# Activation of the last chunk by halves, and q of blocks 3, 5 and 7 transposed by VectorE and two trips through memory

## The chip, the core and the metric

One core of a Trainium2 chip runs the whole program. The metric is the device time of one execution in microseconds (us); the median of three runs of the kernel before is 1563.25 us.

## What is computed

Linear attention over 8 batches of 8 heads, 576 positions each, and then two dense blocks on its 4608 tokens, all in float32:

```python
q_s = exp(q - max(q, -1)); q_s = q_s / (sum(q_s, -1) + 1e-09)      # over the 64 columns of a head
k_s = exp(k - max(k,  2)); k_s = k_s / (sum(k_s,  2) + 1e-09)      # over the positions
attn = einsum('bhsd,bhde->bhse', q_s, einsum('bhsd,bhse->bhde', k_s, v))
x = attn.transpose(0, 2, 1, 3).reshape(4608, 512)
g = relu(x @ w_in) ** 2;  x = g @ w_out                            # first layer, 512 -> 2048 -> 512
h = x @ w2_in;  g = where(h > 0, h, exp(min(h, 0)) - 1);  out = g @ w2_out   # second layer
```

## The kernel before

Tokens go through the first layer in nine blocks of 512 (numbers 0 to 8). A block is *prepared* (its q normalised, transposed, multiplied with the small k-v products of its batches), then its *up* products are computed (16 chunks j, 12 matmuls each), while the preparation of the next block runs beside them in small steps. From block 1 on two blocks form a pair: after the second (even) block's up products follows the pair's *down* product, by a scheme with seven products of quarters instead of eight, cut into 56 *units* of 6 matmuls. A unit u reads its weights from a tile `w1_<t>_<u>` (line 743), which SyncE (SP) loads from the tensors `w1s` in DRAM. Those are written during blocks 1 and 2 by ScalarE and VectorE steps `s_hi` and `s_lo`, whose results `shwo`, `slwo` go out by DMAs on GpSimd's queue (lines 203 and 216), eight groups of four, the group of quarter 3 last. Every float32 operand is split into a high and a low part (ScalarE writes the high one, VectorE the difference: `uh`, `ul` for units, `dh`, `dl` in the second layer), and each product takes three matmuls.

The order is written out by hand. `attention(t)` lists the steps of a block's preparation in numbered slots 0 to 31; `place_all` spreads those slots over the up chunks and units in which they run. For an odd block t, slots 0 and 1 run in the last chunk of block t-2, slots 2 to 22 in chunks 0 to 13 of block t-1, and slots 23 to 31 in units 11 to 21 of the pair t-2, t-1. In q's preparation `q_load` brings 128 tokens, `q_max` to `q_norm` normalise them, `x_tr` transposes them on TensorE (four 128x128 transposes per two heads, line 399, into PSUM), ScalarE copies the result out to `qt` (line 408), and `x_mm` multiplies it with the k-v products (line 427). Tiles come from pools with a given number of buffers; which buffer a new tile gets, and so what its first writer waits for, is settled when the program is built.

In the second layer, tokens go in groups n = 0 to 4 (512, 512, 512, 384 and 384 columns per half). A group's up stage (line 926) leaves its values in eight chunks m, each with rows r = 0 and 1 and two sides; `elu_1` to `elu_5` apply the activation to both sides of a row at once. Then follows the down stage (line 1031): for each step q `d_mm` runs two products, `t2_sum` forms differences of quarters, and `d_split` cuts the operand for step q + 2. The differences T3 and T1 of the last two chunks (number 3) feed the steps 6 and 7.

Of the kernel before, what the change touches and what calls it, by code (L numbers as in the profile page):

```python
# [8 lines left out]
F32 = mybir.dt.float32  # L9
# [3 lines left out]
AF = mybir.ActivationFunctionType  # L13
# [3 lines left out]
P = 128  # L17
# [3 lines left out]
def tile_attention_moe_moe2(  # L21
# [18 lines left out]
    nc = tc.nc  # L40
    NT, DM = q.shape
    B, NP, _, S = kt_dram.shape
    SC = v.shape[3]
    NFC = wi0.shape[0]
    D = 64
    H = DM // D
    TB = 512
    NB = NT // TB
    NS = TB // P
    LAG = 2  # L50
    NSL = 2 * NFC
    PAIRED = 1
# [6 lines left out]
    att = att_pool.__enter__()  # L59
# [7 lines left out]
    dram = ctx.enter_context(tc.tile_pool(name="dram", bufs=1, space=bass.MemoryType.DRAM))  # L67

    x2d = [dram.tile([NP, P, TB], F32, name=f"x2d{t}") for t in range(NB)]
    NG, HW = NFC // 2, DM // 2  # L70
    w2s = [dram.tile([P, 7, 2, HW], F32, name=f"w2s{j}") for j in range(NG)]
    w1s = [dram.tile([P, 7, 2, HW], F32, name=f"w1s{j}") for j in range(NG)]
    w3s = [dram.tile([P, 7, 2, HW], F32, name=f"w3s{j}") for j in range(NG)]

    keep.tile([P, 32], F32, tag="even", name="even")
    ident = att.tile([P, P], F32, tag="ident", name="ident")
# [9 lines left out]
    def xf_slot(i, name):  # L86

        return keep.tile([P, 2 * TB], F32, tag=f"xf{i}", name=name)
# [137 lines left out]
    st = {}  # L226
# [105 lines left out]
    def kv_inv(b, p):  # L332
        z = st["kz", b, p]
        nc.vector.reciprocal(z, z)

    def q_load(t, s):
        qr = att.tile([P, H, D], F32, tag="q", bufs=4, name=f"q{t}_{s}")
        r = t * TB + s * P
        nc.sync.dma_start(qr.rearrange("p h d -> p (h d)"), q[r : r + P, :])
        st["q", t, s] = qr  # L340

    def per_head(ap):
# [45 lines left out]
    def pieces(t):  # L388
        lo, hi = t * TB, (t + 1) * TB
        while lo < hi:  # L390
            b = lo // S
            n = min(hi, (b + 1) * S) - lo
            yield b, lo - t * TB, n
            lo += n

    def x_tr(t, p):
        pt = bank([P, TB], f"pt{t}_{p}")
# [51 lines left out]
    def plan():  # L449
        slots = [[] for _ in range(NSL)]  # L450

        def put(i, f, *a):
            slots[i].append((f, a))

        return slots, put

    def attention(t):

        slots, put = plan()
        new = [b for b, _, _ in pieces(t) if b not in begun]  # L460
        begun.update(new)

        far = t > 1
        for b in new:
            for p in range(NP):
                for i, f in (
                    (0, kt_load), (2, k_max), (5, k_load), (5, v_load), (8, k_row), (8, k_sub), (9 + far, k_exp),
                    (11 + far, kv_mm), (11 + far, kv_sum), (11 + far, kv_inv), (11 + 2 * far, kv_out),
                ):
                    if p == NP - 1 and (f is kv_out if far else i == 11):  # L470
                        i = 12
                    put(i + 4 * p, f, b, p)
        for s in range(NS):
            put(s // 2, q_load, t, s)
            for i, f in (
                (2, q_max), (3, q_sub), (4 + far, q_exp), (5 + 2 * far, q_sum), (6 + 2 * far, q_eps),
                (7 + 2 * far, q_inv), (7 + 2 * far, q_norm),
            ):
                put(i + 5 * s, f, t, s)
        turns = ((25, 28), (26, None), (29, 31), (30, None)) if far else ((25, 27), (26, None), (28, 29), (28, None))  # L480
        for p, (i, j) in enumerate(turns):
            if j is not None:
                put(j, x_mm, t, p)
            put(i, x_tr, t, p)
        return slots
# [305 lines left out]
    def u_out(t, i, side, half, block, m):  # L791

        o = parts_y[i][m]
        nc.vector.tensor_tensor(o, o, accs[side, m], op=ALU.add)
        nc.gpsimd.dma_start(x2d[block][2 * half + m], o)
# [40 lines left out]
    SIZES = (512, 512, 512, 384, 384)  # L836
# [101 lines left out]
    acc, part, g2, es = {}, {}, {}, {}  # L938
# [12 lines left out]
        nc.scalar.activation(p, acc[CHAIN[i], m], AF.Copy)  # L951
        part[i, m] = p

    def rows(m, r):
        return g2[r, m // 2][:, m % 2].rearrange("p s t -> p (s t)")

    def h_part(n, m, r, side, i, add):
# [6 lines left out]
        else:  # L964
            nc.vector.tensor_tensor(h, part[add, m], acc[CHAIN[i], m], op=ALU.add)

    def elu_1(n, m, r):


        e = pool2.tile([P, 2 * SIZES[n]], F32, tag="e", bufs=2, name=f"e{n}_{m}_{r}")  # L970
        nc.scalar.activation(e, rows(m, r), AF.Relu, scale=-1.0)
        es[m, r] = e

    def elu_2(n, m, r):
        e = es[m, r]
        g = pool2.tile([P, 2 * SIZES[n]], F32, tag="g", bufs=2, name=f"t{n}_{m}_{r}")
        nc.scalar.activation(g, e, AF.Tanh, scale=-0.5)
        es[m, r] = e, g

    def elu_3(n, m, r):  # L980
        e = es[m, r][0]
        nc.scalar.activation(e, e, AF.Exp, scale=-1.0)

    def elu_4(n, m, r):
        e, g = es[m, r]
        nc.vector.scalar_tensor_tensor(g, e, 1.0, g, ALU.add, ALU.mult)  # L986

    def elu_5(n, m, r):
        g, h = es.pop((m, r))[1], rows(m, r)
        nc.vector.scalar_tensor_tensor(h, h, 0.0, g, ALU.max, ALU.add)  # L990


# [76 lines left out]
    def second_layer():  # L1069


        nonlocal pool2
        for m in range(2):
            u_out(NB - 2, 4, 0, 1, NB - 2, m)
        early2.tile([P, 56], F32, tag="even", name="even")
        layer_pool.__exit__(None, None, None)
        square_pool.__exit__(None, None, None)
        pool2 = ctx.enter_context(tc.tile_pool(name="pool2", bufs=1, reuse_waits="tile"))
        last = len(SIZES) - 1
        for n in range(last + 1):  # L1080
            steps = {}

            def put(key, f, *a):
                steps.setdefault(key, []).append((f, (n, *a)))

            evict = {
                0: (keep_part, 0), 3: (keep_part, 3), 2: (keep_part, 2), 1: (h_part, 0, 0, 1, 0),
                6: (h_part, 0, 1, 6, 2), 4: (h_part, 1, 1, 4, 3), 5: (h_part, 1, 0, 5, None),
            }
            for at, m, i in ORDER:  # L1090
                put(at, evict[i][0], m, *evict[i][1:])
            if n:
                put(1, lambda n: d_out(n - 1, 4, 0, 1, 0))
            for m in range(NG):
                for x, (to, f, r) in enumerate((
                    (6, elu_1, 0), (7, elu_2, 0), (8, elu_3, 0), (9, elu_4, 0), (10, elu_5, 0), (10, elu_1, 1),
                    (11, elu_2, 1), (12, elu_3, 1), (13, elu_4, 1), (14, elu_5, 1),
                )):
                    put(7 * m + to if m < NG - 1 else ("d", (0, 0, 0, 1, 1, 1, 2, 2, 3, 3)[x]) if x else 56, f, m, r)
            for k in range(3):  # L1100
                put(14 * k + 22, t2_sum, "T3", k)
                put(14 * k + 25 if k < 2 else ("d", 0), t2_sum, "T1", k)
            put(30, d_split, 0)
            put(39, d_split, 1)
            put(54, d_split, 2)
            for q, f, *a in (
                (4, t2_sum, "T3", 3), (5, t2_sum, "T1", 3),
                (6, d_keep, 4, 0, "e"), (8, d_v), (10, t2_sum, "T2", 0), (11, t2_sum, "T2", 1),
                (12, d_keep, 0, 0, "g"), (12, t2_sum, "T2", 2), (13, t2_sum, "T2", 3), (16, d_keep, 6, 1, "g"),
                (19, t2_sum, "T4", 0), (20, d_out, 6, 0, 0, 1), (21, d_out, "v", 0, 1, 1), (22, t2_sum, "T4", 1),  # L1110
                (23, t2_sum, "T4", 2), (24, t2_sum, "T4", 3), (25, d_out, 0, 1, 0, 0),
            ):
                put(("d", q), f, *a)
            if n < last:
                for q, f, a in (
                    (6, x2_sum, "T3"), (7, x2_sum, "T1"), (9, x2_split, 0), (14, x2_sum, "T2"), (15, x2_split, 1),
                    (16, x2_split, 6), (17, x2_split, 2), (18, x2_split, 3), (25, x2_sum, "T4"), (26, x2_split, 4),
                    (27, x2_split, 5),
                ):
                    steps.setdefault(("d", q), []).append((f, (n + 1, a)))  # L1120
                for k, (side, h) in enumerate(((0, 0), (1, 0), (1, 1), (0, 1))):
                    steps.setdefault(35 + 2 * k, []).append((x2_load, (n + 1, h, side)))
            for at, m, i in ORDER:
                take(n, m, i)
                run(steps.get(at, ()))
            for q in range(NU // 2):
                d_mm(n, 2 * q)
                d_mm(n, 2 * q + 1)
                run(steps.get(("d", q), ()))
                if 0 < q < NU // 2 - 2:  # L1130
                    d_split(n, q + 2)
        d_out(last, 4, 0, 1, 0)
# [6 lines left out]
    def run(steps):  # L1139
        for f, a in steps:  # L1140
            f(*a)
# [3 lines left out]
    with tc.manual_schedule():  # L1145
# [25 lines left out]
        x = attention(PAIRED + 1)  # L1171
# [3 lines left out]
        for t in range(PAIRED, NB - 2, 2):  # L1175
            seconds = [(t, "s", s) for s in range(NU // 2)]
            x = attention(t + 2)
# [3 lines left out]
            x = attention(t + 3)  # L1181
# [14 lines left out]
        at = 0  # L1196
# [14 lines left out]
        at = 0  # L1211
# [134 lines left out]
```

## Time and profile before

| | |
|---|---|
| median of three runs | 1563.25 us (1563.06 to 1564.92) |
| profiled execution, its own time | 1561.17 us |
| span of its instructions | 1559.0 us |
| TensorE (PE) busy | 1533.3 us, 98% |
| VectorE (DVE) busy | 1227.1 us, 79% |
| ScalarE (ACT) busy | 1013.2 us, 65% |
| GpSimd (POOL) busy | 129.3 us, 8% |
| transfers | 351.66 MB, mean 226 GB/s |

The profile names an instruction by its line, engine and operation, and by the tiles it writes and reads. Idle time is put down to whatever the instruction behind it waited for.

### The profile page before, as it was taken

The numbers are of one execution on the slowest core, as the hardware profiler recorded it, in microseconds if no ns is written. First come the engines' busy times: TensorE is split into PE (matmuls) and PEld (weight loads), VectorE is DVE, ScalarE is ACT, GpSimd is POOL, SyncE is SP. The second block draws the span as 40 slices with busy tenths as digits, with TensorE's granted clock in tenths as the row PEclk, the third lists the DMA queues.
The fourth block names the chain that finished last, engine by engine and source line by source line (L and its number), as shares of the span: only waits on it lengthen the run. The fifth ranks groups of instructions, "written<-read, shape, count | busy, mean of one in ns | idle before, by whom it ended". The sixth has DMA issues, their size and how long they took to land.

```text
span 1559.0 us, 25506 instructions
## 1 busy us (share of the span) xinstructions
PE 1533.3 (98%) x9056; PEld 1321.1 (85%) x9056; DVE 1227.1 (79%) x1793; ACT 1013.2 (65%) x1606; POOL 129.3 (8%) x202
## 2 busy tenths in 40 slices
PE   7999999999999999999999999999999999999999
PEld 5778777878778787787888889988998899999998
DVE  8998597787778787885686888688868886887876
ACT  7886655577565765656564876387538853864863
POOL 1002220032011310032201000000000000000000
PEclk9999999999999999999999999999999999999999
DMA  9857566677586775855686776877686768888876
GB/s 268 244 168 257 203 220 210 225 256 259 152 273 212 266 227 170 265 183 186 215 272 204 206 233 179 241 202 237 179 241 194 231 180 250 275 256 281 261 237 206
DMA packets 200765, 351.66 MB, mean 226 GB/s; under 512 B 20160, under 2 KB 67264, under 8 KB 200640
## 3 DMA queue, kind: packets, MB, share of 16 engines
q1 hardware_dynamic: 186096, 302.71, 64.1%
q0 software_dynamic: 14400, 47.20, 7.6%
q8 instruction: 73, 1.20, 0.3%
q14 instruction: 52, 0.43, 0.1%
q10 hardware_dynamic: 144, 0.13, 0.0%
HBM read 287.05 MB, written 62.91 MB: 224 GB/s over the span
## 4 chain that ended last, share of the span: by engine, by line
PE 75%; DVE 10%; issue 6%; ACT 5%; DMA 3%; POOL 1%; SPq 0%; ACTq 0%; DVEq 0%; POOLq 0%
PE p L926 21%; PE y L1031 17%; PE p L765 16%; PE ph L648 6%; PE ph L649 6%; PE ph L650 6%; DVE dl L1012 2%; ACT dh L1011 1%; DMA kt<-kt_dram 1%; DVE ul L753 1%; PE px L427 1%; DVE g L990 1%; PE pk L307 1%; DVE t L986 1%; PE pt L399 1%
## 5 line engine op out<-in xcount | busy, mean ns | idle before, releaser
L1031 PE MATMUL y<-w,dh 128*128 128x256 f32 x2016 | 359.2, 281 | 0.0
L926 PE MATMUL p<-x2h,w 128*128 128x512 f32 (+1 forms) x1120 | 321.6, 367 | 0.0
L1031 PEld LDWEIGHTS y<-w,dh 128*128 128x128 f32 x2016 | 309.7, 188 | 0.1
L1031 PE MATMUL y<-w,dl 128*128 128x256 f32 x1008 | 285.1, 283 | 4.9 <-DVE dl L1012 4.7
L765 PE MATMUL p<-uh,w 128*128 128x512 f32 x896 | 282.6, 392 | 0.3 <-DMA w<-w1s 0.3
L648 PE MATMUL ph<-xh,wi0h 128*128 128x512 f32 x576 | 229.5, 399 | 0.0
L926 PEld LDWEIGHTS p<-x2h,w 128*128 128x128 f32 x1120 | 207.1, 188 | 26.1
L650 PE MATMUL ph<-xh,wi0l 128*128 128x512 f32 x576 | 224.8, 390 | 2.6 <-DVE wi0l L149 2.6
L649 PE MATMUL ph<-xl,wi0h 128*128 128x512 f32 x576 | 225.1, 391 | 0.7 <-DVE xl L586 0.6
L926 PE MATMUL p<-x2l,w 128*128 128x512 f32 (+1 forms) x560 | 205.5, 367 | 0.0
L765 PEld LDWEIGHTS p<-uh,w 128*128 128x128 f32 x896 | 168.2, 188 | 37.1 <-issue 1.5
L1031 PEld LDWEIGHTS y<-w,dl 128*128 128x128 f32 x1008 | 189.7, 188 | 8.0 <-DVE dl L1012 7.8
L1011 ACT ACTIVATE dh<-g 128x1024 fp32r<-128x1024 f32 (+1 forms) x120 | 115.8, 973 | 114.0 <-PE y L1031 101.2
L752 ACT ACTIVATE uh<-B 128x512 fp32r<-128x512 f32 x192 | 120.4, 631 | 93.7 <-PE p L765 70.3
L765 PE MATMUL p<-ul,w 128*128 128x512 f32 x448 | 176.4, 394 | 2.0 <-DVE ul L753 1.6
L753 DVE TENSOR_TENSOR ul<-B,uh 128x512 fp32r<-128x512 f32 x192 | 129.5, 688 | 47.1 <-ACT uh L752 46.4
L1012 DVE TENSOR_TENSOR dl<-g,dh 128x1024 fp32r<-128x1024 f32 (+1 forms) x120 | 133.8, 1116 | 39.1 <-ACT dh L1011 38.8
L657 ACT ACTIVATE B<-ph 128x512 f32<-128x512 f32 x128 | 76.3, 596 | 120.6 <-PE ph L650 116.8
L648 PEld LDWEIGHTS ph<-xh,wi0h 128*128 128x128 f32 x576 | 109.0, 189 | 28.4 <-issue 3.9
L650 PEld LDWEIGHTS ph<-xh,wi0l 128*128 128x128 f32 x576 | 108.2, 188 | 27.3 <-DVE wi0l L149 4.1
L649 PEld LDWEIGHTS ph<-xl,wi0h 128*128 128x128 f32 x576 | 108.2, 188 | 22.7 <-DVE xl L586 1.8
L926 PEld LDWEIGHTS p<-x2l,w 128*128 128x128 f32 x560 | 105.1, 188 | 13.0
(155 smaller groups left out, 2279.8 us busy)
## 6 DMA issues: line engine op xcount, KB each, us to landing
w<-w2s SPq DMA_DIRECT2D x280, 256.0 KB, 3.2
w<-w3s SPq DMA_DIRECT2D x280, 256.0 KB, 3.0
w<-w1s SPq DMA_DIRECT2D x224, 256.0 KB, 3.8
raw_wo<-wo_dram SPq DMA_DIRECT2D x32, 512.0 KB, 4.6
vr<-v_dram SPq DMA_DIRECT2D x32, 320.0 KB, 5.6
kt<-kt_dram SPq DMA_DIRECT2D x32, 288.0 KB, 4.0
q<-q_dram SPq DMA_DIRECT2D x36, 256.0 KB, 4.5
ks<-k_dram SPq DMA_DIRECT2D x28, 320.0 KB, 4.6
```

The costliest lines, as they stand in the source:

```text
L307: nc.tensor.matmul(pk[j * D : (j + 1) * D], ks[:, c, j * D : (j + 1) * D], vr[:, c, j * (D + 1) : (j + 1) * (D + 1)], start=(c == 0), stop ...
L648: nc.tensor.matmul(ph, hi[:, c], xh[p], start=(p == 0), stop=False)
L649: nc.tensor.matmul(ph, hi[:, c], xl[p], start=False, stop=False)
L650: nc.tensor.matmul(ph, lo[:, c], xh[p], start=False, stop=(p == NP - 1))
L657: nc.scalar.activation(g, ph, AF.Relu)
L752: nc.scalar.activation(hi, x, AF.Copy)
L753: nc.vector.tensor_tensor(lo, x, f32(hi), op=ALU.subtract)
L765: nc.tensor.matmul(accs[side, m], w[:, s, m], x, start=(new and (j, s) == (0, 0) and x is hi), stop=(j == NG - 1 and s == 1), skip_group_c ...
L926: nc.tensor.matmul(acc, w[:, s, c], x[:, k], start=(begin and (k, s) == (0, 0) and x is hi), stop=((k, s) == (1, 1)), skip_group_check=not ...
L1011: nc.scalar.activation(hi, x, AF.Copy)
L1012: nc.vector.tensor_tensor(lo, x, f32(hi), op=ALU.subtract)
L1031: nc.tensor.matmul(y2[side, b][:, a * HW : (a + 1) * HW], x[:, u % 2, at], w[:, s], start=(new and (j, s, a) == (0, 0, 0) and x is hi), st ...
```

## The change

The last chunk's activation is split: in chunk 7 row 1 is taken in two halves, first the side that T3 needs, then the other one; row 0 stays whole. T3 and T1 of the last chunks are formed two steps earlier. In blocks 3, 5 and 7 the 16 transposes on TensorE and the four copies out of PSUM are gone. VectorE turns 32x32 squares of each normalised quarter into the tile `q<t>` (written with a step of four elements), four DMAs of 32 partitions each put that tile into a DRAM tensor `qd<t>` in the order wanted, and two DMAs read it back into the buffers xf0 and xf1. Quarters are loaded with every fourth token, in buffers that the `qt` tiles have otherwise (two instead of four), and each step of q's preparation runs earlier, so that the last quarter is done in chunk 12 of the even block.

```diff
+    TURNED = range(PAIRED + 2, NB, 2)
+    qd = {t: dram.tile([2, 2, P, TB], F32, name=f"qd{t}") for t in TURNED}
...
     def q_load(t, s):
...
+        rows = q[t * TB : (t + 1) * TB]
+        if t in TURNED:
+            qr = att.tile([P, H, D], F32, tag="qt", bufs=2, name=f"q{t}_{s}")
+            rows = rows.rearrange("(p s) c -> s p c", s=NS)[s]
+        else:
+            qr = q_tile(t)[:, s * DM : (s + 1) * DM].rearrange("p (h d) -> p h d", d=D)
+            rows = rows[s * P : (s + 1) * P]
+        nc.sync.dma_start(qr.rearrange("p h d -> p (h d)"), rows)
...
+    def q_turn(t, s):
+        turned = q_tile(t).rearrange("p (g t s) -> p g t s", g=2 * H, s=NS)[:, :, :, s]
+        nc.vector.transpose(turned, st.pop(("q", t, s)).rearrange("p h (j d) -> p (h j) d", j=2))
+
+    def q_store(t):
+        n = D // 2
+        for i in range(P // n):
+            rows = qd[t].rearrange("h u (r d) n -> d (h u r) n", d=n)[:, :, i * P : (i + 1) * P]
+            nc.gpsimd.dma_start(rows, q_tile(t)[i * n : (i + 1) * n].rearrange("p (g n) -> p g n", n=P))
+
+    def q_rows(t, half):
+        x = xf_slot(half, f"qt{t}_{half}").rearrange("p (u n) -> p u n", u=2)
+        nc.gpsimd.dma_start(x, qd[t][half].rearrange("u p n -> p u n"))
...
+            if t in TURNED:
+                at = (0, 4, 9, 13)[s]
+                put((0, 0, 8, 12)[s], q_load, t, s)
+                for i, f in (
+                    (2, q_max), (3, q_sub), (4, q_exp), (6, q_sum), (7, q_eps), (7, q_inv), (8, q_norm), (8, q_turn),
+                ):
+                    put(at + i, f, t, s)
+                continue
...
+        if t in TURNED:
+            put(21, q_store, t)
+            for half in range(2):
+                put(24, q_rows, t, half)
+                put(29 + 2 * half, x_mm, t, 2 * half)
+            return slots
...
-                    put(7 * m + to if m < NG - 1 else ("d", (0, 0, 0, 1, 1, 1, 2, 2, 3, 3)[x]) if x else 56, f, m, r)
+                    if m < NG - 1:
+                        put(7 * m + to, f, m, r)
+                    elif r:
+                        put((55, 55, 56, ("d", 0), ("d", 0))[x - 5], f, m, r, 1)
+                        put(("d", (1, 2, 2, 4, 4)[x - 5]), f, m, r, 0)
+                for to, f in zip((0, 0, 0, 1, 1), (elu_1, elu_2, elu_3, elu_4, elu_5)):
+                    if m == NG - 1:
+                        put(("d", to), f, m, 0)
...
-                (4, t2_sum, "T3", 3), (5, t2_sum, "T1", 3),
+                (2, t2_sum, "T3", 3), (3, t2_sum, "T1", 3),
```

On GpSimd's queue, at the end of block 2, the DMAs `w1s<-shwo` and `w1s<-slwo` of groups 2 and 3 (the last of the eight) stand so in the kernel before, and after them the next pair's results:

```order
L203 DMA w1s_100<-shwo_2_2_2388 128x2x256
L216 DMA w1s_100<-slwo_2_2_2391 128x2x256
L203 DMA w1s_101<-shwo_3_1_2499 128x2x256
L216 DMA w1s_101<-slwo_3_1_2502 128x2x256
L203 DMA w1s_101<-shwo_3_2_2528 128x2x256
L216 DMA w1s_101<-slwo_3_2_2531 128x2x256
L795 DMA x2d_82<-k_1_0_2713 128x512
```

The same place now, with block 3's four stores to `qd` and its two reads:

```order
L205 DMA w1s_100<-shwo_2_2_2392 128x2x256
L218 DMA w1s_100<-slwo_2_2_2395 128x2x256
L416 DMA qd_114<-q_2202 32x16x128 x4
L205 DMA w1s_101<-shwo_3_1_2507 128x2x256
L218 DMA w1s_101<-slwo_3_1_2510 128x2x256
L205 DMA w1s_101<-shwo_3_2_2534 128x2x256
L218 DMA w1s_101<-slwo_3_2_2537 128x2x256
L420 DMA qt_0_2765<-qd_114 128x2x512
L420 DMA qt_1_2767<-qd_114 128x2x512
```

The four stores have moved in ahead of the four DMAs of group 3, whose last one unit 3 of the first pair reads.

On SP, the loads of the weights of units 2 to 6 of that pair, with the semaphores that each waits for, before:

```order
L743 DMA w_1_2_2534<-w1s_100 128x512 [waits DMASW6_49,DMASW5_49,DMASW7_49,DMASW1_49,DMAHW6_49,DMASW0_49,DVE_49]
L743 DMA w_1_3_2536<-w1s_101 128x512 [waits DMASW3_49,DMASW2_49,DMASW4_49,DMASW1_49,DMAHW7_49,DMASW0_49,DVE_49]
L743 DMA w_1_4_2577<-w1s_102 128x512 [waits DMAHW0_49,PE_49]
L743 DMA w_1_5_2579<-w1s_103 128x512 [waits DMAHW1_49]
L743 DMA w_1_6_2581<-w1s_104 128x512 [waits DMAHW2_49,PE_49]
```

And now:

```order
L785 DMA w_1_2_2540<-w1s_100 128x512 [waits DMASW6_49,DMASW5_49,DMASW7_49,DMASW1_49,DMAHW6_49,DMASW0_49,DVE_49]
L785 DMA w_1_3_2542<-w1s_101 128x512 [waits DMAHW6_49,DMASW7_49,DMAHW7_49,DMASW6_49,PE_49]
L785 DMA w_1_4_2583<-w1s_102 128x512 [waits DMAHW0_49]
L785 DMA w_1_5_2585<-w1s_103 128x512 [waits DMAHW1_49]
L785 DMA w_1_6_2587<-w1s_104 128x512 [waits DMAHW2_49]
```

The load for unit 3 had a buffer that a `shwo` tile left; in the new program its tile lies at the address of unit 2's tile, and the load waits for unit 2's load and for TensorE (DMAHW6 and PE) besides the two stores it reads.

On VectorE, at the start of a down stage of the second layer (group 0; `t_7_r`, `g` are the activation of the last chunk, `dl_q` the low part for step q), before:

```order
L1004 TENSOR_TENSOR g_0_2_9219<-g_0_2_9219 128x2x512
L986 SCALAR_TENSOR_TENSOR t_7_0_9558<-e_7_0_9526,t_7_0_9558 128x1024
L990 SCALAR_TENSOR_TENSOR g_0_3_9402<-g_0_3_9402,t_7_0_9558 128x1024
L1012 TENSOR_TENSOR dl_3_9595<-g_0_0_8881,dh_3_9594 128x1024
L1012 TENSOR_TENSOR dl_4_9630<-g_0_1_9044,dh_4_9629 128x1024
L986 SCALAR_TENSOR_TENSOR t_7_1_9626<-e_7_1_9592,t_7_1_9626 128x1024
L990 SCALAR_TENSOR_TENSOR g_0_3_9403<-g_0_3_9403,t_7_1_9626 128x1024
L1012 TENSOR_TENSOR dl_5_9666<-g_0_2_9219,dh_5_9665 128x1024
L1004 TENSOR_TENSOR t_0_3_9697<-g_0_3_9403,g_0_3_9402 128x1024
L1012 TENSOR_TENSOR dl_6_9700<-t_0_3_9697,dh_6_9699 128x1024
```

And now:

```order
L1030 SCALAR_TENSOR_TENSOR t_7_1_9458<-e_7_1_9456,t_7_1_9458 128x512
L1034 SCALAR_TENSOR_TENSOR g_0_3_9343<-g_0_3_9343,t_7_1_9458 128x512
L1048 TENSOR_TENSOR g_0_2_9159<-g_0_2_9159 128x2x512
L1030 SCALAR_TENSOR_TENSOR t_7_0_9505<-e_7_0_9503,t_7_0_9505 128x1024
L1034 SCALAR_TENSOR_TENSOR g_0_3_9342<-g_0_3_9342,t_7_0_9505 128x1024
L1056 TENSOR_TENSOR dl_3_9542<-g_0_0_8821,dh_3_9541 128x1024
L1048 TENSOR_TENSOR t_0_3_9576<-g_0_3_9343,g_0_3_9342 128x1024
L1056 TENSOR_TENSOR dl_4_9579<-g_0_1_8984,dh_4_9578 128x1024
L1048 TENSOR_TENSOR g_0_3_9342<-g_0_3_9342 128x2x512
L1056 TENSOR_TENSOR dl_5_9614<-g_0_2_9159,dh_5_9613 128x1024
```

Two instructions of half size now stand ahead of `dl_3`, and the differences T3 and T1 (the L1048 rows behind it) come two steps of `dl` earlier than they did.

## Rows read from the trace of the kernel before

**Rows 1.** The page: busy time, share of the span and instructions of each engine.

```profile
PE 1533.3 (98%) x9056; PEld 1321.1 (85%) x9056; DVE 1227.1 (79%) x1793; ACT 1013.2 (65%) x1606; POOL 129.3 (8%) x202
```

**Rows 2.** Waits of PE: who waited for whom, us in total, times, longest.

```profile
PE y L1031 <- DVE dl L1012: 4.7, 12, 0.5
...
PE p L765 <- DMA w<-w1s: 0.3, 1, 0.3
```

**Rows 3.** Line 399: count, ns min/median/max, first and last start.

```profile
L399 PE MATMUL pt<-ident,q x128: 271/272/328, 99.5 to 715.1; 128*128 128x128 f32 x128
```

**Rows 4.** Timeline of PE around eight transposes: start, us, engine, line, operation.

```profile
257.04 0.39 PE L765 MATMUL p<-uh,w 128*128 128x512 f32 x1
257.27 1.04 PE L399 MATMUL pt<-ident,q 128*128 128x128 f32 x8
...
258.38 0.40 PE L765 MATMUL p<-ul,w 128*128 128x512 f32 x1
```

**Rows 5.** Waiting chain at the first pair's start, in order of time.

```profile
224.81 2.51 DMA w1s<-slwo
...
227.85 2.80 DMA w<-w1s
...
230.78 9.38 PE p L765 x40
```

**Rows 6.** Timeline of POOL there: first and last of four DMAs.

```profile
221.66 0.72 POOL L203 DMA_DIRECT2D w1s<-shwo  x1 [7.99 <-ACT shwo L202]
...
224.81 0.74 POOL L216 DMA_DIRECT2D w1s<-slwo  x1
```

**Rows 7.** Timeline of PE there: last matmul of unit 2.

```profile
230.09 0.39 PE L765 MATMUL p<-uh,w 128*128 128x512 f32 x1
```

**Rows 8.** Groups by line and form: busy us, mean ns of one, idle before.

```profile
L216 POOL DMA_DIRECT2D w3s<-slwo x24 | 17.5, 730 | 15.1 <-DVE slwo L215 7.7 <-DVE sumswo L175 6.8 <-issue 0.2
...
L795 POOL DMA_DIRECT2D x2d<-k x18 | 10.0, 554 | 223.6 <-DVE k L794 222.8 <-issue 0.3
...
L352 DVE TENSOR_TENSOR q<-q,qm 128x512 f32<-128x512 f32 x32 | 21.9, 684 | 0.2
...
L1004 DVE TENSOR_TENSOR g<-g,g 128x1024 f32<-128x1024 f32 x24 | 29.3, 1219 | 0.1
```

**Rows 9.** Timeline of DVE in block 2: instructions behind idle time.

```profile
191.16 0.69 DVE L661 TENSOR_TENSOR B<-B 128x512 f32<-128x512 f32 x1 [2.29 <-ACT B L657]
...
208.36 0.69 DVE L215 TENSOR_TENSOR slwo<-sumswo,shwo 128x512 fp32r<-128x512 f32 x1 [0.86 <-ACT shwo L202]
...
221.29 0.69 DVE L215 TENSOR_TENSOR slwo<-sumswo,shwo 128x512 fp32r<-128x512 f32 x1 [0.17 <-ACT shwo L202]
```

**Rows 10.** The page: DMA issues, count, KB each, us to landing.

```profile
vr<-v_dram SPq DMA_DIRECT2D x32, 320.0 KB, 5.6
...
q<-q_dram SPq DMA_DIRECT2D x36, 256.0 KB, 4.5
ks<-k_dram SPq DMA_DIRECT2D x28, 320.0 KB, 4.6
```

**Rows 11.** Timeline of DVE, first down stage of the second layer.

```profile
925.74 1.23 DVE L990 SCALAR_TENSOR_TENSOR g<-g,t 128x1024 f32<-128x1024 f32 x1
926.88 1.22 DVE L1012 TENSOR_TENSOR dl<-g,dh 128x1024 fp32r<-128x1024 f32 x1
```

**Rows 12.** Timeline of PE in the same stage: steps 3 and 6.

```profile
928.39 0.28 PE L1031 MATMUL y<-w,dl 128*128 128x256 f32 x1
...
936.75 0.39 PE L1031 MATMUL y<-w,dh 128*128 128x256 f32 x2
937.60 0.39 PE L1031 MATMUL y<-w,dl 128*128 128x256 f32 x1 [0.45 <-DVE dl L1012]
```

**Rows 13.** Timeline of PE in group 3's down stage: step 3.

```profile
1379.75 0.39 PE L1031 MATMUL y<-w,dh 128*128 128x256 f32 x2
1380.24 0.39 PE L1031 MATMUL y<-w,dl 128*128 128x256 f32 x1
```

More of the change, by code (lines that the diff above doesn't have):

```diff
@@ L334, in kv_inv, with q_tile @@
         nc.vector.reciprocal(z, z)
+    def q_tile(t):
+        if ("all", t) not in st:
+            st["all", t] = att.tile([P, NS * DM], F32, tag="q", name=f"q{t}")
+        return st["all", t]
     def q_load(t, s):
-        qr = att.tile([P, H, D], F32, tag="q", bufs=4, name=f"q{t}_{s}")
-        r = t * TB + s * P
-        nc.sync.dma_start(qr.rearrange("p h d -> p (h d)"), q[r : r + P, :])
+        rows = q[t * TB : (t + 1) * TB]
[6 more added lines that the diff above has]
+        nc.sync.dma_start(qr.rearrange("p h d -> p (h d)"), rows)
         st["q", t, s] = qr
@@ L394, in pieces @@
             lo += n
+    def q_turn(t, s):
[9 more added lines that the diff above has]
+        nc.gpsimd.dma_start(x, qd[t][half].rearrange("u p n -> p u n"))
+        for i in range(2):
+            st["qt", t, 2 * half + i] = x[:, i]
     def x_tr(t, p):
@@ L952, in keep_part, with rows @@
         part[i, m] = p
-    def rows(m, r):
+    def rows(m, r, *side):
+        if side:
+            return g2[r, m // 2][:, m % 2, side[0]]
         return g2[r, m // 2][:, m % 2].rearrange("p s t -> p (s t)")
@@ L965, in h_part, with elu_1, elu_2, elu_3 @@
             nc.vector.tensor_tensor(h, part[add, m], acc[CHAIN[i], m], op=ALU.add)
[L967 to L976, printed above, removed]
+    def elu_1(n, m, r, *side):
+        e = pool2.tile(list(rows(m, r, *side).shape), F32, tag="e", bufs=2, name=f"e{n}_{m}_{r}")
+        nc.scalar.activation(e, rows(m, r, *side), AF.Relu, scale=-1.0)
+        es[m, r, *side] = e
+    def elu_2(n, m, r, *side):
+        e = es[m, r, *side]
+        g = pool2.tile(list(rows(m, r, *side).shape), F32, tag="g", bufs=2, name=f"t{n}_{m}_{r}")
         nc.scalar.activation(g, e, AF.Tanh, scale=-0.5)
-        es[m, r] = e, g
-    def elu_3(n, m, r):
-        e = es[m, r][0]
+        es[m, r, *side] = e, g
+    def elu_3(n, m, r, *side):
+        e = es[m, r, *side][0]
         nc.scalar.activation(e, e, AF.Exp, scale=-1.0)
-    def elu_4(n, m, r):
-        e, g = es[m, r]
+    def elu_4(n, m, r, *side):
+        e, g = es[m, r, *side]
         nc.vector.scalar_tensor_tensor(g, e, 1.0, g, ALU.add, ALU.mult)
-    def elu_5(n, m, r):
-        g, h = es.pop((m, r))[1], rows(m, r)
+    def elu_5(n, m, r, *side):
+        g, h = es.pop((m, r, *side))[1], rows(m, r, *side)
         nc.vector.scalar_tensor_tensor(h, h, 0.0, g, ALU.max, ALU.add)
```

## The prediction, as it was put on record before the run

> **What bounds the kernel now.** I read the page's table of engines first: TensorE (PE) is busy in 98% of the span, VectorE (DVE) in 79%, ScalarE (ACT) in 65%, GpSimd (POOL) in 8% [rows 1]. Then PE's waits: nearly all of what the trace calls waiting there is 12 times 0.4 us for a `dl` of DVE in the second layer's down stages, and once 0.3 us for a weight load, the one of unit 3 of the first pair [rows 2]. So nothing is gained by relieving an engine other than PE. A gain comes from work that leaves PE or from those two waits; a loss comes from a new wait of PE. The sum has three terms: the transposes, the activation by halves, and what the new work on DVE, POOL and the queues does to PE.
>
> **Term 1, the transposes.** Eight blocks have 128 of them, 16 a block [rows 3], so three blocks lose 48. The 271 ns of a row is latency, since they overlap. What they take from the stream is seen between neighbours: the matmul ahead starts at 257.04 and the first transpose at 257.27, so a matmul of 512 columns takes a step of 0.23; from the first transpose to the next matmul are 1.11 us [rows 4], and 1.11 less one such step is 0.88 for eight, 0.11 us each (the last step counted as a full one is my choice; without it the price is 0.14). 48 x 0.11 = **-5.2 us** (-6.7 at 0.14). The 12 copies on ACT that go with them cost nothing today, because ACT has a third of its time free.
>
> **Term 2, the activation by halves.** Before the split, DVE runs without a break into `dl_3`: the last `g` begins at 925.74, `dl_3` at 926.88 and ends at 928.10 [rows 11]; PE uses it first at 928.39 [rows 12]. That is 0.3 us of slack. In the new order two instructions of 128x512 stand ahead of it. The nearest row of that size takes 0.68, half of a 128x1024 row is 0.61 [rows 8]; I take 0.6 each, so `dl_3` is 1.2 us late less some 0.2-0.3 of slack: about 1.0 us of new wait in each of the three groups of 512 columns. In the groups of 384 the slack is gone already: at step 3 two matmuls take 0.49 from the first one's start to the `dl` matmul [rows 13], which is a step of about 0.12 each plus 0.25 of lateness; an instruction pair there is shorter (three quarters, 0.95), so the wait becomes 1.2. New: 3 x 1.0 + 2 x 1.2 = 5.4 us. What goes: the steps 5 to 7 get their T3 and T1 two `dl` earlier, so I let all old waits go: 4.7 [rows 2], and with each a small part that the trace does not count (936.75 plus two steps of 0.12 is 936.99, the `dl` matmul starts at 937.60 [rows 12]: 0.61 lost where 0.45 is shown, 0.16 more), 12 x 0.16 = 1.9, in all 6.6. Net **-1.2 us**, which I round with the shorter 384 groups to -1.5. Bounds: -6.6 if ACT had been what held DVE and step 3 does not stall; +1 if old waits at steps 6 and 7 keep 2 of the 6.6.
>
> **Term 3, the first pair's start.** This is where the change can hurt. Unit 3's weights come by a chain: DVE's last `slwo` at 221.29 [rows 9]; POOL's four DMAs from 221.66, behind 7.99 us of idle time, to the last at 224.81 [rows 6]; that one lands 2.5 us later; SP issues the load at 227.85, which takes 2.8; PE goes on at 230.78, 0.3 late [rows 5]. The chain has no reserve: any delay of it is a wait of PE. Two things are put into it.
>
> DVE. Ahead of its last `slwo` now stand four turns of block 3 and the sum, eps, inverse and norm of its last quarter. A turn is not in the trace: the nearest rows of the same size are 0.68 (128x512) and 1.22 (128x1024, which stands for a slow one) [rows 8]. I take 0.7, 2.8 in all, and 1.6 for the other four by the first of these rows and smaller ones. DVE's idle time in that stretch is 2.29, 0.86 and 0.17 in the rows where it is seen [rows 9]; on the other hand the quarter loads 2 and 3 must wait for a turn to free their buffer, and a load of q lands 4.5 us after its issue [rows 10], which I charge with 1 us more. 2.8 + 1.6 + 1 less 2.4 of idle time: DVE ends 3 us later, at about 224.2 (222.3 where it absorbs all but 1 us; 226.6 with turns of 1.22).
>
> POOL. Its four stores stand ahead of group 3's four DMAs, and the first one waits for the last turn. A DMA of 128 runs holds POOL for 0.55, one of 256 runs for 0.73 [rows 8]; 0.18 per 128 runs makes 0.55 + 3 x 0.18 = 1.08 for a store's 512 runs, and twice 0.73 = 1.46 is its upper end. 4 x 1.08 = 4.3, so 228.5; three of the four DMAs at 0.73 follow, and the last one starts at about 230.7 instead of 224.8. It lands after 2.5, SP takes 0.5, the load 2.8, and I add 1 for the 1 MB of `qd` reads beside it: PE goes on at 237.5 to 237.7 instead of 230.78, **+7 us** with rounding. Nothing covers it: PE has the work of units 0 to 2 only, which ends at 230.32 (the last matmul at 230.09 [rows 7] and a step of 0.23), and no other stream of PE's stands ahead of unit 3 that could be drawn in.
>
> The bounds of this term. From below it cannot be nothing: the load for unit 3 has unit 2's buffer now, so it cannot start before 230.32, and 230.32 + 0.5 + 2.8 = 233.7, +2.9 us, even if DVE and POOL are in time. From above: turns at 1.22 (+2.4), stores at 1.46 (+1.5), and runs of 512 bytes that land slower. For the last, a load of `vr` with 640 shorter runs lands 5.6 us after its issue, `ks` with the same 320 KB 4.6 [rows 10]; 1 us for 640 runs is 3.2 for the 2048 runs of the four stores, if the small DMAs must pass behind them. Together 7 + 2.4 + 1.5 + 3.2 = +14.
>
> [...] No row before shows a DVE instruction that writes with a step; I used the row of dense 128x512. [...]
>
> **The other places.** In pairs 2 and 3 the same stores stand in POOL's queue, but no weights are written any more, so only block 5's and 7's own reads wait for them; `x_mm` follows many units later. I cost it at nothing, covered by those units of PE; if the cover were gone, the wait would be a store, a read and two landings, 4 x 1.1 + 0.6 + 2 x 2.5 = 10 us, against some 19 us from the read's slot to its use, by my reading of the slots. The turns in these pairs stand on DVE ahead of `ul` parts; DVE's 21% of free time [rows 1] hides 0.7 us each, and 8 x 0.7 = 5.6 us if it did not. The transfers grow by 2 MB a block, 6 MB on 352: no wait of PE is on a queue there.
>
> **Sum.** -5.2 - 1.5 + 7.0 = +0.3 us. The profiled execution took 1561.17, a span of 1559.0 and 2.17 around it; so 1561.5 for it. The median of the runs is 2.08 above the profiled execution, which gives 1563.6; I put down **1563.5**. Within 0.2% (3.1 us) a measurement of this kernel can hardly tell a change from none, so this counts as no change.
>
> **Rivals.** *Faster: the first pair's chain copes.* If DVE's idle time takes the turns and POOL hands the stores out in 0.55 each, as a DMA of 128 runs, the stores cost 2.2 us that fall into the 7.99 us in which POOL idles [rows 6]; only the buffer wait of 2.9 stays. -5.2 - 1.5 + 2.9 = -3.8, 1559.5. If the waits of the second layer go as a whole, 5.1 less again, 1554.4. For it: the 8 us of idle POOL; against it: the last turn can't come before that idle time is nearly over, since the last quarter's load and normalisation come first.
>
> *Slower: POOL's queue holds up group 3's DMAs.* One mechanism, the same place: the stores wait for slow turns, and each handed-out run costs time. With turns of 1.22, stores of 1.46 and half of the slower landing, the wait is 7 + 2.4 + 1.5 + 1.6 = 12.5: -5.2 - 1.5 + 12.5 = +5.8, 1569. It decides from a wait of 9.8 us on (6.7 gained and 3.1 to be seen). For it: the idle time of 0.17 before the last `slwo` [rows 9] shows that DVE is the late one there already; against it: 128 runs more cost POOL only 0.18.
>
> *The gain is only the transposes*: step 3's new waits eat all that the later steps give back, and the first pair's wait is 5; -5.2 + 5 = -0.2, 1563. It can't be told from my forecast by the time, only by the profile, and is counted with it.
>
> **How the numbers follow.** 0.48 for my forecast with the last case, whose own range is 1560.3 to 1566.5; 0.29 for faster; 0.23 for slower. The range of 8 in 10 leaves out about one in ten on each side: from 1556, most of the faster case, to 1569, the slower one's middle.
>
> **What would show it.** The list by line should have 80 transposes. PE should stand idle once in the first pair, ahead of unit 3, until about 237 with a `w1s` load named; with POOL's four stores in the rows before it at 1.1 each, and the four `w1s` DMAs behind them. The turn's own row tells 0.7 from 1.22. In the second layer, the `dl` waits should stand at step 3, about 1 us each, and none at 6 and 7. My forecast is wrong if unit 3 starts before 234, if it starts after 241, or if step 3 is on time.

## The result and the profile after

The changed kernel takes 1583.21 us, median of four runs (1581.93 to 1586.33), against 1563.15 for the kernel before: ratio 1.0136, 95% interval 1.0123 to 1.0149. It is 20 us slower, where I forecast 1563.5 and no change. Its profiled execution has a span of 1581.2 us.

The table of engines after, against [rows 1]:

```profile
PE 1533.7 (97%) x9008; PEld 1320.8 (84%) x9008; DVE 1239.8 (78%) x1815; ACT 1009.3 (64%) x1609; POOL 140.2 (9%) x220
```

TensorE has 48 instructions fewer and is busy as long as before: against the 5.2 us of work that I priced them at stand 7.6 us at a lower clock (below). The waits of PE after the start-up (from 190 us on), against [rows 2]: who waited for whom, us in total, times, longest.

```profile
PE p L807 <- DMA w<-w1s: 14.3, 1, 14.3
PE y L1075 <- DVE dl L1056: 5.1, 5, 1.2
PE pk L309 <- ACT ks L300: 4.9, 2, 2.6
PE ph L690 <- ACT B L699: 2.7, 1, 2.7
PE p L807 <- DVE ul L795: 0.9, 2, 0.5
```

Three new things stand there: 14.3 us ahead of unit 3, where I put 7; five waits of 1 us in the down stages, as forecast; and three waits of 2.6, 2.7 and 2.4 us (7.7 in all) in blocks 2, 4 and 6 that no sentence of the prediction has.

Behind unit 3's wait and the three smaller ones the trace shows TensorE at work with a granted clock of 0.5 in place of 1.0, which I call half clock. Windows of 2 us around unit 3's wait: busy time of PE, PEld, DVE, ACT, POOL with instructions, granted clock, share of the DMA engines, GB/s.

```profile
234.00:236.00 2.00, 0.89 (x4) 0.39 (x3) 1.97 (x3) 1.26 (x2) 0.65 (x1) 1.00 0.33 74
...
238.00:240.00 2.00, 0.00 (x0) 0.00 (x0) 0.11 (x1) 0.00 (x0) 0.83 (x2) 0.51 0.66 145
...
250.00:252.00 2.00, 2.00 (x7) 1.52 (x6) 0.00 (x0) 0.00 (x0) 0.00 (x0) 0.50 1.03 357
...
256.00:258.00 2.00, 2.00 (x11) 1.64 (x10) 1.05 (x3) 0.89 (x2) 0.72 (x1) 1.00 0.61 152
```

In two busy microseconds seven matmul records stand where eleven stand a little later. Added up in windows of 1 us (busy time times what the clock lacks of 1), 3.0 us are lost here and 1.6, 1.5 and 1.6 behind the three smaller waits: 7.6 us before rounding.

The start-up, which no edit touches, ends up to 5 us earlier or later from one profiled execution to the next (the landmark below is at 140.61 us in e3 and at 145.68 in e2). So I compare profiles from a landmark, the first k-v product (`pk`) after 140 us, the same matmul in every kernel. Before and after:

```profile
141.22 0.80 PE L307 MATMUL pk<-vr,ks 128*64 128x65 f32 x20
```

```profile
141.58 0.80 PE L309 MATMUL pk<-vr,ks 128*64 128x65 f32 x20
```

From there to the end of the span are 1417.8 us before and 1439.6 after: 21.8 more. The terms: unit 3's wait +14.0 (14.3 less the 0.3 of before), the three waits +7.7, half clock +7.6, the waits for `ul` -0.7, and, at the prices that I forecast, the transposes -5.2 and the activation -1.5 (e10 and e1 below bear them out). Sum +21.9.

**Where unit 3's wait comes from.** GpSimd after, against [rows 6]: start, us, operation, and in brackets its idle time before.

```profile
227.44 0.69 POOL L416 DMA_DIRECT2D qd<-q  x1 [10.15 <-DVE sumswo L181]
230.81 0.66 POOL L416 DMA_DIRECT2D qd<-q  x1 [2.69 <-issue]
234.15 0.65 POOL L416 DMA_DIRECT2D qd<-q  x1 [2.67 <-issue]
237.46 0.66 POOL L416 DMA_DIRECT2D qd<-q  x1 [2.66 <-issue]
238.11 0.72 POOL L205 DMA_DIRECT2D w1s<-shwo  x1
240.90 0.72 POOL L218 DMA_DIRECT2D w1s<-slwo  x1 [2.08 <-issue]
241.61 0.71 POOL L205 DMA_DIRECT2D w1s<-shwo  x1
242.32 0.72 POOL L218 DMA_DIRECT2D w1s<-slwo  x1
```

It is the chain that I drew, the stores ahead of the four weight DMAs. But a store that counts 0.66 us as busy holds the queue for 3.34: behind it stand 2.67 us that belong to no wait the profile knows ("issue"). The last weight DMA starts at 242.3 where I had 230.7, and PE goes on at 249.2 where I had 237.5. Of the 11.6 us at that DMA, 3.2 stand ahead of the first store (the last turn ends at 227.0 and the store starts at 227.4, where I had 224.2), and 8.4 in the queue: from the first store to the last weight DMA are 14.9 us where I had 6.5.

The kernel before has such a wait too. Where four weight DMAs of 256 runs stand close together in block 2, the fourth starts 2.1 us late:

```profile
189.45 0.72 POOL L216 DMA_DIRECT2D w1s<-slwo  x1 [2.10 <-DVE mt_wo L156]
```

VectorE had given its `slwo` at 187.0, so the releaser named is not what held it; in e12 below, with twice the room, this wait is gone.

**Where the three waits come from.** A turn on VectorE in block 2, and SyncE's queue behind it (start, time of issuing, what):

```profile
203.72 1.09 DVE L410 STREAM_TRANSPOSE q<-q 128x512 f32<-128x512 f32 x1
```

```profile
204.83 0.33 SPq L351 DMA_DIRECT2D q<-q_dram  x1
205.21 1.65 SPq L223 DMA_DIRECT2D w1s<-wo  x3
```

The load of q goes out right after the turn's end (203.72 + 1.09 = 204.81), which frees its buffer, and the weights, `ks` and `vr` come behind it. The same three DMAs of the weights in the kernel before:

```profile
199.07 2.16 SPq L221 DMA_DIRECT2D w1s<-wo  x3
```

They were issued 6.1 us earlier (5.8 from the landmark). What stands late in ScalarE's order in blocks 2, 4 and 6:

```profile
209.09 0.60 ACT L699 ACTIVATE B<-ph 128x512 f32<-128x512 f32 x1 [3.10 <-DMA w1s<-wo]
...
407.38 0.65 ACT L122 ACTIVATE raw_wi<-raw_wi 128x512 f32<-128x512 f32 x1 [5.65 <-DMA raw_wi<-wi_dram]
...
592.58 0.63 ACT L368 ACTIVATE q<-q 128x512 f32<-128x512 f32 x1 [2.52 <-DVE q L364]
```

In blocks 2 and 4 ScalarE waits, by the profile, for DMAs of the weights that went out behind a quarter of q; in block 6 it waits for VectorE to give it the quarter itself. Behind each of the three, in ScalarE's order, stands the `ks` or the eviction `B` that PE waits for. The data of `ks` is not late: in block 2 VectorE was done with it at 203.1, and ScalarE came to it at 210.3.

### The profile page after: what moved, and what is told of

It is laid out like the page before. It is cut to its first block, busy times and chain, and to the rows that moved or that the text cites. A ratio compares the mean times of both kernels' runs of the same rounds, so it can differ in the third digit from the quotient of the medians.

```text
span 1581.2 us, 25483 instructions
## 1 busy us (share of the span) xinstructions
PE 1533.7 (97%) x9008; PEld 1320.8 (84%) x9008; DVE 1239.8 (78%) x1815; ACT 1009.3 (64%) x1609; POOL 140.2 (9%) x220
## 4 chain that ended last, share of the span: by engine, by line
PE 74%; DVE 10%; issue 5%; ACT 5%; DMA 3%; POOL 1%; SPq 0%; POOLq 0%; DVEq 0%; ACTq 0%
PE p L968 20%; PE y L1075 20%; PE p L807 17%; PE ph L690 5%; PE ph L691 5%; PE ph L692 5%; PE px L455 1%; DVE g L1034 1%; DVE t L1030 1%; DVE dl L1056 1%; DVE ul L795 1%; DMA raw_wi<-wi_dram 1%; PE pk L309 1%; DMA vr<-v_dram 1%; DVE T L775 1%
## 5 line engine op out<-in xcount | busy, mean ns | idle before, releaser
L807 PE MATMUL p<-uh,w 128*128 128x512 f32 x896 | 282.1, 394 | 14.3 <-DMA w<-w1s 14.3
L690 PE MATMUL ph<-xh,wi0h 128*128 128x512 f32 x576 | 231.3, 402 | 2.7 <-ACT B L699 2.7
L1030 DVE SCALAR_TENSOR_TENSOR t<-e,t 128x1024 f32<-128x1024 f32 (+3 forms) x85 | 89.9, 1058 | 33.7 <-ACT e L1026 33.4
```

The source lines that it names most:

```text
L690: nc.tensor.matmul(ph, hi[:, c], xh[p], start=(p == 0), stop=False)
L807: nc.tensor.matmul(accs[side, m], w[:, s, m], x, start=(new and (j, s) == (0, 0) and x is hi), stop=(j == NG - 1 and s == 1), skip_group_c ...
```

## The experiments

Theory A: the loss is in two queues, GpSimd's behind stores of many runs and SyncE's behind loads that wait for a turn. Rival B: VectorE is too full with the turns, whatever the queue. The changed kernel is the basis unless said.

**e1_elu**, the activation by halves alone:

```diff
-    TURNED = range(PAIRED + 2, NB, 2)
+    TURNED = range(0)
```

> Only the activation by halves; q of all blocks is transposed on TensorE as before. Both theories give the term of the prediction: five waits of about 1 us for the low part at step 3, 5.1 in all, in place of twelve of 0.4 with 1.9 beside them, so 1.5 us less than before, 1561.7. A rival that the halves cost something elsewhere would show 1563 or more.

1561.37 us, ratio 0.9983 (0.9972 to 0.9993). From the landmark (143.91) to the end of its span (1560.2) are 1416.3 us, 1.5 less than before. The `dl` waits:

```profile
PE y L1075 <- DVE dl L1056: 5.1, 5, 1.1
```

The term is right in sign, size and place.

**e2_queue**, two of the four loads on another queue:

```diff
-        nc.sync.dma_start(qr.rearrange("p h d -> p (h d)"), rows)
+        queue = nc.gpsimd if t in TURNED and s > 1 else nc.sync
+        queue.dma_start(qr.rearrange("p h d -> p (h d)"), rows)
```

> The changed kernel, with the third and fourth quarter's loads of the turned blocks on GpSimd's queue instead of SyncE's. Theory A (those loads wait on SyncE's queue for a turn to free their buffer, and the loads of k, v and raw weights stand behind them): the three waits of TensorE in blocks 2, 4 and 6 (2.6, 2.7, 2.4) go, and the 4.7 us of half clock behind them; 1583.2 - 12.4 = 1571, and the wait ahead of unit 3 stays at 14 or more. Rival B (VectorE, with turns of 1.1 us and the steps of q moved forward, is late for k's preparation whatever the queue): the three waits stay, 1581 to 1585.

1580.72 us, 1.0106 (1.0085 to 1.0126): 2.5 less than the changed kernel, not 12.4 (5.6 less from the landmark, which its profiled execution reached 4.1 us later). Waits of PE from 190 us on:

```profile
PE p L808 <- DMA w<-w1s: 16.0, 1, 16.0
...
PE pk L309 <- ACT ks L300: 3.4, 2, 2.6
PE ph L691 <- ACT B L700: 1.3, 1, 1.3
```

In block 2 the wait of 2.6 is gone and one of 1.3 stands later, in block 4 one of 0.8 stands in place of 2.7, but block 6's went from 2.4 to 2.6, and PE, earlier at unit 3, waited 1.7 longer there. The time at half clock costs 2.2 us in place of 7.6. So SyncE's queue was a part of the three waits and not the whole.

**e3_late**, the stores behind unit 1:

```diff
-            put(21, q_store, t)
...
             place_all(x[2:10], seconds[13:20])
+            place(seconds[0], q_store, t + 2)
```

> The changed kernel, with the four stores of a turned block behind unit 1 of the pair, and so behind group 3's weight DMAs in GpSimd's queue. Theory A (GpSimd is held for 3.3 us by each store of 512 runs, and group 3's DMAs stand behind): the wait of 14.3 ahead of unit 3 falls to about 1.3 (last low part of the weights at 229.6, 0.7, 2.5 to land, 0.5, 2.8 to load: 236.2 against unit 2's end at 234.9) and with it the 2.9 of half clock: about 1567. Rival B (VectorE's turns make the last low part late, the stores add little): 5 us or more of the wait stay, 1573 or more.

1568.37 us, 1.0034 (1.0024 to 1.0045). Unit 3's wait is 1.7 us; the three others stay (2.7, 2.7, 2.4):

```profile
PE pk L309 <- ACT ks L300: 5.1, 2, 2.7
PE ph L689 <- ACT B L698: 2.7, 1, 2.7
PE p L806 <- DMA w<-w1s: 1.7, 1, 1.7
```

With one line moved 15 us come back. For unit 3 theory A holds, and B, which left 5 us or more of the wait, falls.

**e4_both**, e2 and e3 together.

> Both edits: the loads of the third and fourth quarter on GpSimd's queue and the stores behind unit 1. Theory A: only the wished terms are left, 5.2 for the transposes and 1.5 for the activation, and 0 to 3 us of wait ahead of unit 3, since VectorE's last low part is still behind four turns: 1556 to 1560, faster than before. Rival B: the turns on VectorE alone cost more than they save, 1565 or more.

1566.82 us, 1.0023 (1.001 to 1.0036): 7 to 11 us short of the expectation. Waits of 1.5, 0.3 and 2.7 us are left in blocks 2, 4 and 6 and 3.0 ahead of unit 3, with 3.1 us of half clock behind block 6's. Block 6, whose wait is the longest of the three, shows why. VectorE, then ScalarE, then PE:

```profile
569.01 0.69 DVE L360 TENSOR_REDUCE qm<-q 128x8 f32<-128x512 f32 x1 [1.11 <-DMA q<-q_dram]
...
571.67 1.08 DVE L411 STREAM_TRANSPOSE q<-q 128x512 f32<-128x512 f32 x1
572.61 0.67 DVE L365 TENSOR_TENSOR q<-q,qm 128x512 f32<-128x512 f32 x1
```

```profile
573.31 0.63 ACT L369 ACTIVATE q<-q 128x512 f32<-128x512 f32 x1 [2.51 <-DVE q L365]
...
575.39 0.60 ACT L699 ACTIVATE B<-ph 128x512 f32<-128x512 f32 x1
...
576.56 0.61 ACT L300 ACTIVATE ks<-ks 128x512 f32<-128x512 f32 x1
```

```profile
577.22 1.35 PE L309 MATMUL pk<-vr,ks 128*64 128x65 f32 x20 [2.65 <-ACT ks L300]
```

On either queue the load cannot begin before a turn has freed one of the two buffers (on SyncE's it went out at 204.83, where a turn ended at 204.81; on GpSimd's here at 564.58, where one ended at 563.89). VectorE's maximum waits in its order for the landing, the turn follows, ScalarE's exponential waits 2.5 us for VectorE, and behind it in ScalarE's order stand the eviction and the `ks` that PE needs. Theory A as I had it was too narrow.

**e9_early**, e4 with more slots between load and use:

```diff
-                at = (0, 4, 9, 13)[s]
-                put((0, 0, 8, 12)[s], q_load, t, s)
+                at = (0, 2, 10, 13)[s]
+                put((0, 0, 8, 10)[s], q_load, t, s)
```

> e4_both, with the second quarter's steps two slots earlier and the fourth quarter's load at slot 10, so that the loads of the third and fourth quarter have 4 and 5 slots before their first use, where they had 3. Theory A, amended (with two buffers a load cannot begin before a turn; VectorE's maximum waits in its order for the landing, and ScalarE's exponential behind it holds the eviction that TensorE waits for): the waits of TensorE in blocks 4 and 6 (0.3 and 2.7) and the half clock behind them (3.1) go, about 1561. Rival B (VectorE is simply too full with the turns): a wait of 2 us or more stays in block 6, 1565 or more.

1561.38 us, 0.9995 (0.9986 to 1.0004). The waits in blocks 2, 4 and 6 are gone (0.3 us left in all), with the same turns on the same engine:

```profile
PE p L807 <- DMA w<-w1s: 3.3, 1, 3.3
...
PE pk L309 <- ACT ks L300: 0.3, 1, 0.3
```

Rival B falls here too, except at unit 3: there 3.3 us stay. VectorE's last `slwo`, behind the turns, starts here 2.8 us later from the landmark than in the kernel before (landmarks 143.56 and 141.22), and so does the last weight DMA:

```profile
228.85 0.69 DVE L217 TENSOR_TENSOR slwo<-sumswo,shwo 128x512 fp32r<-128x512 f32 x1
```

```profile
223.72 0.68 DVE L215 TENSOR_TENSOR slwo<-sumswo,shwo 128x512 fp32r<-128x512 f32 x1
```

The load of unit 3's weights also takes 3.8 us in place of 2.8; what slows it was not tried.

**e5_dense and e6_runs** measure the turn and the store by themselves.

```diff
-        turned = q_tile(t).rearrange("p (g t s) -> p g t s", g=2 * H, s=NS)[:, :, :, s]
+        turned = q_tile(t).rearrange("p (s g t) -> p s g t", g=2 * H, s=NS)[:, s]
```

> The changed kernel, with the turned squares written densely, not with a step of four elements (q of the turned blocks is then in a wrong order). If the step makes the turn slow, it falls from 1.09 us to about 0.68, the row of 128x512; if the transposition itself is slow, it stays near 1.09. The time by either: 1581 to 1584.

A single run, 1581.36 us. The turn in the changed kernel and here (count, busy us, mean ns):

```profile
L410 DVE STREAM_TRANSPOSE q<-q 128x512 f32<-128x512 f32 x12 | 13.2, 1101 | 0.4
```

```profile
L410 DVE STREAM_TRANSPOSE q<-q 128x512 f32<-128x512 f32 x12 | 8.5, 711 | 0.4
```

The dense turn took 0.71 us, about what the row of that size takes (0.68 [rows 8]); written with a step of four floats, 16 bytes, it took 1.10, 0.39 us more. With the shorter turns the waits in blocks 2, 4 and 6 are 2.3, 2.2 and 1.6, and unit 3's is 14.6: the turn's own price is the smaller part of the loss.

```diff
-            rows = qd[t].rearrange("h u (r d) n -> d (h u r) n", d=n)[:, :, i * P : (i + 1) * P]
-            nc.gpsimd.dma_start(rows, q_tile(t)[i * n : (i + 1) * n].rearrange("p (g n) -> p g n", n=P))
+            rows = qd[t].rearrange("h u (r d) n -> (h u r d) n", d=4)[i * P : (i + 1) * P].rearrange("(p r) n -> p (r n)", r=4)
+            nc.gpsimd.dma_start(rows, q_tile(t)[i * n : (i + 1) * n])
```

> The changed kernel, with each store written as 32 runs of 8 KB in place of 512 runs of 512 bytes (the order in memory is then wrong). Theory A (GpSimd is held by the number of runs): from one store to the next 0.6 to 0.8 us instead of 3.34, unit 3's wait falls from 14.3 to 3 to 5, about 1570. Rival (held by the bytes, or by the transfer itself): the steps between stores stay above 2 us, and the wait above 8.

A single run, 1574.52 us. The four stores follow one another without a gap, and unit 3's wait falls to 6.8, not to 3 to 5:

```profile
229.00 1.98 POOL L416 DMA_DIRECT2D qd<-q  x4 [9.82 <-DVE sumswo L181]
230.97 0.76 POOL L205 DMA_DIRECT2D w1s<-shwo  x1
...
237.49 0.73 POOL L218 DMA_DIRECT2D w1s<-slwo  x1 [4.30 <-DVE T L775]
```

The bytes are the same, so between the stores it is the number of runs that held GpSimd. What is left of the wait stands ahead of the last weight DMA, 4.3 us, though VectorE had given its `slwo` at 231.3. That this is the same wait for room as in e12 is likely, but not shown.

**e12_scratch**, twice the room for GpSimd's DMAs:

```diff
-    nc = bacc.Bacc("TRN2", target_bir_lowering=False, num_devices=1, dynamic_dma_scratch_size=1024)
+    nc = bacc.Bacc("TRN2", target_bir_lowering=False, num_devices=1, dynamic_dma_scratch_size=2048)
```

> The changed kernel, with 2048 in place of 1024 bytes for GpSimd's DMAs in the launch. If a store of 512 runs holds GpSimd because it waits for room, the idle time of 2.67 us behind each store falls to about half or less, and the wait ahead of unit 3 by 4 us or more; if it is the making of the runs, both stay (2.67 and 14.3).

A single run, 1575.2 us, unit 3's wait 6.1. With all 512 runs three stores now follow one another at 0.66 us, and the fourth waits 1.6:

```profile
228.29 1.97 POOL L416 DMA_DIRECT2D qd<-q  x3 [10.73 <-DVE sumswo L181]
231.84 0.66 POOL L416 DMA_DIRECT2D qd<-q  x1 [1.59 <-issue]
```

And the weight DMA in block 2 that stood idle for 2.1 us in the kernel before (189.45), and in the changed kernel too (190.29), follows without a gap:

```profile
188.63 0.71 POOL L218 DMA_DIRECT2D w1s<-slwo  x1
```

With 1024 bytes each store starts 3.3 to 3.4 us after the one ahead of it; here the fourth starts 3.55 us after the first. So the 2.67 us are not the making of the runs: they go with the room. That the queue waits there for room is how I read it; no row names it.

**e8_swap**, e1 with the operand cut ahead of the activation in steps 1 to 4:

```diff
+                if 0 < q < 5:
+                    d_split(n, q + 2)
                 run(steps.get(("d", q), ()))
-                if 0 < q < NU // 2 - 2:
+                if 4 < q < NU // 2 - 2:
                     d_split(n, q + 2)
```

> Only the activation by halves, as in e1_elu, and in the down stage's steps 1 to 4 the cut of the operand for step q + 2 comes ahead of the activation's and the sums' instructions. Theory (VectorE's low part of step 3 is late because of what stands ahead of it): the five waits of 1 us fall to nearly nothing, 4.5 us less than e1_elu, about 1557. Rival (ScalarE, which gives the high part behind the activation's three passes, sets it): the waits stay at 3 us or more in all, 1560 or more.

1557.11 us, 0.9969 (0.9958 to 0.998). Of 5.1 us of `dl` waits 0.7 are left:

```profile
PE y L1075 <- DVE dl L1056: 0.7, 2, 0.3
```

**e11_three**, e9 with that order.

> e9_early with the order of e8_swap in the down stages; three blocks turned. Theory: the five waits of 1 us go, 4.4 less than e9_early's 1561.4: 1557; the wait of 3.3 us ahead of unit 3 and 1.5 of half clock stay. Rival (the two orders disturb one another): 1560 or more.

1557.49 us, 0.9967 (0.9955 to 0.9979), as expected: the two edits add. Unit 3's wait is 3.9.

**e10_two**, that order and e9's steps, with blocks 5 and 7 alone turned, and their stores in the place that the change gave them.

```diff
-    TURNED = range(PAIRED + 2, NB, 2)
+    TURNED = range(PAIRED + 4, NB, 2)
```

> e8_swap, with only blocks 5 and 7 turned on VectorE (the loads of the third and fourth quarter on GpSimd's queue and the steps as in e9_early; stores where the change put them). No weight of the pairs is written behind those stores. Theory: 32 transposes at 0.11 us less than e8_swap, 3.5 us, and no new wait: 1553.6. Rival (the turn's price is on VectorE in every block): nothing gained on e8_swap, 1557 or more.

1552.72 us, 0.9945 (0.9933 to 0.9958): 9.5 us less than the kernel before beside it (1562.23), the fastest of all. From the landmark (141.52) to the end (1550.9) are 1409.4 us; e8 has 1412.7 (142.20 to 1554.9). 3.3 us for 32 transposes is 0.10 each (by the medians 4.4 us, 0.14). The stores, in their old place, make no wait where no weights stand behind them. All waits of PE from 190 us on:

```profile
PE p L808 <- DVE ul L796: 0.9, 2, 0.5
PE y L1076 <- DVE dl L1057: 0.7, 2, 0.3
PE pk L309 <- ACT ks L300: 0.2, 1, 0.2
PE pt L428 <- DVE q L399: 0.2, 1, 0.2
```

## Why the prediction was wrong

*Term 1, the transposes: right.* I had -5.2 at 0.11 each; e10 against e8 gives 0.10 by the landmark and 0.14 by the medians. The page's list has 80 of them at that line.

*Term 2, the activation: right.* -1.5, with the new waits at step 3 (forecast 5.4, measured 5.1) and none at steps 6 and 7. e8 shows the cause by taking it away. What I did not ask is whether the order had to be so: `dl_3` needs nothing of the activation, and cut earlier it frees another 4 us.

*Term 3, unit 3: the mechanism right, the size wrong.* I had +7 and an upper end of 14; it is +14.0, and 3.0 of half clock behind it. The failed step is "0.18 per 128 runs makes 0.55 + 3 x 0.18 = 1.08 for a store's 512 runs". I drew a line through two busy times (128 and 256 runs), and what a store costs the queue is not in its busy time but in the idle time behind it, 2.67 us. The trace of the kernel before held that wait already (2.1 us at 189.45), in a row that I did not draw on. e3, e6 and e12 take away the place, the runs and the lack of room, each by itself, and each time more than half of the wait goes. The turn at 0.7 was a smaller error (1.10): with the step it takes 1.10 and without it 0.71 (e5), and I took the dense row. I also misread [rows 9]: the `slwo` at 221.29 that I called the last is the last but one, and the last starts at 223.72. From the landmark the two come 5.5 and 4.9 us later in the changed kernel, where I had 3. The whole chain is 18.1 us late; PE's own losses in block 2 put it 4.1 us later at unit 3 and hide that much. My lower bound of 2.9 from the shared buffer was never what ended the wait: where the stores stood ahead (the changed kernel, e6 and e12), the load began when the weights had landed, after unit 2's end (245.2 against 234.9 in the changed kernel).

*Where I cost nothing: wrong.* "The transfers grow by 2 MB a block, 6 MB on 352: no wait of PE is on a queue there" and the 1 us that I charged for quarters that "must wait for a turn to free their buffer". I counted the wait for the quarter itself, not what stands behind it: on SyncE's queue the DMAs of the weights (seen in the trace; e2 takes 3.1 of 5.3 us away in blocks 2 and 4 and nothing in block 6), and in VectorE's and ScalarE's order everything behind the maximum and the exponential (e4; e9 takes it away). 7.7 us of waits and 4.7 of half clock.

*The half clock: not in the sum.* 7.6 us, a third of the loss. After the start-up the longest wait of the kernel before is 0.5 us [rows 2], and none of its windows of 1 us from 80 to 1540 us shows a granted clock below 1.00.

*The rivals.* The slower one named the place but was priced by the same 1.46 at most for a store; 1569 was 14 us short. The "coping" rival failed at the same step. With the two things set right (e9) the change takes as long as the kernel before, its interval holding 1. e11 is faster by the order of e8, and e8 alone has the same time (1557.11 against 1557.49). Of what was tried, the turns gain only with block 3 left to TensorE (e10), 4.4 us on e8: the idea was sound for two blocks of three, and its places were not.

*Still open.* Some waits of about 2.6 us are followed by half clock and others are not: in the changed kernel all three, in e2 the one of 2.6 us in block 6 is not, in e4 the one of 2.65 in the same block is, and the one of 3.0 ahead of unit 3 is not. No run here tells what decides it. Nor did I try block 3 with its turns placed behind VectorE's last `slwo`, which by e9 is what remains between three turned blocks and two.

## What to carry to other kernels

A DMA's price on its queue is the distance to the next one (3.34 us for a store here), not its busy time (0.66), and a line through two short ones (0.55 and 0.73, which gave 1.08) says nothing of a longer one; idle time behind several short ones in a row can show it (2.1 us at 189.45). Before a load's buffer is made to wait for a later step, list what stands behind it in its queue and what stands behind its first reader on that engine; here those cost 7.7 us of waits and 4.7 of half clock, more than all that the change saved (6.7). A wait of a few microseconds on a full TensorE is to be priced with the time at half clock that can follow it: 1.5 to 1.6 us behind waits of 2.4 to 2.7 in the changed kernel, 3.0 behind the one of 14.3.

## What the hardware showed

A store of 512 runs held GpSimd's queue for 3.34 us with 1024 bytes of room and for 0.66 (three of four) with 2048; of 32 runs, for 0.50 with 1024. Four DMAs of 256 runs in a row held it for 2.1 us ahead of the fourth with 1024 bytes, and not in the same place with 2048. A 32x32 transposition of 128x512 floats took 0.71 us written densely and 1.10 written with a step of four. TensorE's granted clock fell to 0.5 in the changed kernel's waits of 2.4 to 2.7 us and of 14.3 us and stayed there for 3 to 6 us of work behind them.
